# A cross network's last layer: residual rows by DMA transposes instead of TensorE transposes, natural row order, and a new order of the last groups

## The chip, the cores and the metric

One core of a Trainium2 chip runs the kernel. The metric is the device time in microseconds of one execution of the whole program. The kernel was already tuned: TensorE is busy for 99% of the span before the change.

## The reference, cut to what matters

```python
B, F, D, L = 16384, 26, 16, 6          # Din = 416
def reference(x0, ws, bs):             # x0 (16384, 416), ws (6, 416, 416), bs (6, 416), all bf16
    x = x0
    for l in range(6):
        proj = jnp.einsum('bd,de->be', x, ws[l]) + bs[l]
        x = x0 * proj + x
    return x
```

Each layer is a 416x416 matrix product, a multiply by the first input and an addition of the previous x (here called the residual).

## The kernel before

The 16384 rows are eight groups of 2048. A group is held transposed: features on the partitions (three tiles of 128 features, `t` = 0, 1, 2, and a tail of 32), rows in the free dimension (four chunks of 512, `j`). The 48 pairs of group and layer are interleaved, so that one pair's TensorE work hides another's eviction. Groups 0 to 6 finish transposed, are turned by DMA transposes and stored.

The last pair, group 7 layer 5, has nothing behind it to hide its end. It is computed "row-major": the data is the stationary operand, the weights stream, and the result has rows on the partitions, ready to store. It goes in four row blocks `kk` of four 128-row pieces `j`. A block is 4 tail matmuls, 4 bias matmuls and 12 main matmuls into four PSUM banks, an eviction on ScalarE, a multiply and an addition on VectorE. The addition needs the residual in row-major form too, and the kernel before makes it with TensorE transposes:

```python
def turn_main(kp, bks, ts):            # 24 transposes of 128x128 for each pair of row blocks, kp = 0, 1
    for j in range(NJ):
        for h2 in range(2):
            for t in ts:
                o = h2 * CH + t * P
                add("pe", ... h.transpose(psum_t(bks[j])[:, o:o + P], xcol(t, j, kk), ident[:, :]) ...)
def rows_out(kp, bks):                 # copies out of PSUM: j == 0 (and j == 2 of kp 1) on ScalarE, others on VectorE
    ...
def nat_mul(kk, j, b):
    ... ScalarE: on[:, j, kk, :] = PSUM bank b
    ... VectorE: on *= x0 rows          # the last piece: one VectorE operation out of PSUM
def nat_add(kk, j):
    ... VectorE: on += x5n[:, j, kk, :]  # the residual rows
# [... cut ...]
turn_main(0, bka, (0, 1)); turn_tails(0, bka)
nat_rows(0, bkb, True)                  # tail and bias matmuls of block 0
for j in range(NJ): nat_full(0, j, bkb[j], False, (0, 1))
turn_main(0, bka, (2,)); rows_out(0, bka)
layer_full(0, bkb, (2,))                # the rest of block 0, with its multiplies and additions
turn_main(1, bka, (0, 1, 2)); turn_tails(1, bka); rows_out(1, bka)
nat_rows(1, bkb, True); layer_full(1, bkb); nat_store(0, 2, 0, NJ)
# [... blocks 2 and 3 alike, with bka and bkb ...]
```

`add` appends to an engine's queue and derives semaphore waits from what an operation reads and writes. Each queue is filled in the order of the `add` calls. Here `bka` and `bkb` are the two halves of the eight PSUM banks. By those waits a write into a bank starts only when the reader of its old contents is done. (PSUM is the memory that TensorE's results go to; the banks are its eight parts.)

Of the kernel before, what the change touches and what calls it, by code (L numbers as in the profile page):

```python
# [3 lines left out]
P = 128  # L4
# [194 lines left out]
def bass_standalone__cross_network_dcn__recsys_kernel(  # L199
# [18 lines left out]
             (0, 4), (1, 3), (2, 2), (3, 1), (0, 5), (1, 4), (2, 3), (3, 2), (4, 0), (1, 5),  # L218
             (2, 4), (3, 3), (4, 1), (5, 0)]
    order += [(NG - 1 - g, L - 1 - l) for g, l in reversed(order)]  # L220
    order[-6:] = [(5, 5), (7, 3), (6, 4), (7, 4), (6, 5), (7, 5)]
    assert len(set(order)) == NG * L
    cuts = [1, 2, 3, 4, 4, 4, 4, 4, 4, 4, 4, 4, 3, 2]
    batches = []
# [94 lines left out]
    def quad(g, l, j):  # L319
        q = (j + turn_of(g, l)) % NJ  # L320
        return q, slice(q * T32, (q + 1) * T32)
# [194 lines left out]
    def perm(ap, j):  # L516
        return ap[j * CH:(j + 1) * CH, :].rearrange("(p k) f -> p k f", k=KK)
# [28 lines left out]
    def psum_t(b):  # L546
        return psum[:, b * CH:(b + 1) * CH].bitcast(BF16)
# [75 lines left out]
    def load_last():  # L623

        for j in range(NJ):
            add("sp", lambda h, j=j: h.dma_start(x0n7[:, j, :, :], perm(rows7, j)),
                writes=(x0_all(sn) + x03_toks(sn) if j == 0 else []) + [("n7", j)], lane="n7", batch=0)
        for j in range(NJ):
            add("sp", lambda h, j=j: h.dma_start(brow[j * T32:j * T32 + 1, :], bs[L - 1:L, :]),
                writes=[("brow", j)] + (["brow"] if j == 0 else []), lane="brow", batch=0)  # L630

    def output(g):

        s, s3 = xset[(g, L)], xtail[(g, L)]
        def turn(t):
            add("sp", lambda h: h.dma_start_transpose(
                ost[:, :, t * P:(t + 1) * P], xs[s][:, t * GC:(t + 1) * GC]),
                reads=[("x", s, t, j) for j in range(NJ)], writes=[("ost", t)], lane="ot", batch=g)

        turn(0)  # L640
        add("sp", lambda h: h.dma_start_transpose(ot3[:, :, :], x3s[s3][:, :]),
            reads=[("x3", s3)], writes=["ot3"], lane="ot3", batch=g)
        add("pool", lambda h: h.tensor_copy(  # L643
            ost[:, :, NT * P:D].rearrange("p (j k) f -> p j k f", j=NJ),
            ot3[:, :, :].rearrange("p k (j f) -> p j k f", j=NJ)),
            reads=["ot3"], writes=[("ost", NT)])
        turn(1)
        turn(2)
        rows = out[g * GC:(g + 1) * GC, :]
        o = ost[:, :, :].rearrange("p (j k) f -> p j k f", j=NJ)  # L650
        parts = [("(j k p) f -> p j k f", 0, NJ)]
        if g == 0:
            parts = [("(j p k) f -> p j k f", 0, NJ)]
        for pat, j0, j1 in parts:
            add("sp", lambda h, pat=pat, j0=j0, j1=j1: h.dma_start(
                rows[j0 * CH:j1 * CH, :].rearrange(pat, j=j1 - j0, k=KK), o[:, j0:j1, :, :]),
                reads=[("ost", t) for t in range(NT + 1)],
                writes=[("out", g, j0)], lane="out", batch=g)
        free_x.append(s)
        free_3.append(s3)  # L660

    items = []
    where = {(b[min(1, len(b) - 1)], 0): b for b in batches[:-1]}
    where[((LAST - 1, L - 1), 0)] = batches[-1]
    del where[((0, 0), 0)]
    where[((0, 1), 0)] = where.pop(((1, 0), 0))
    tiles = [((1, 0), 0), ((1, 0), 1), ((0, 1), 0), ((0, 1), 1), ((0, 1), 2), ((1, 0), 2)]
# [1 line left out]
    for jb, i in tiles:  # L669
        items.append(("tile", jb, i))  # L670
        if (jb, i) in where:
            items.append(("tails", where[(jb, i)]))

    late = items.index(("tile", (LAST, L - 2), NT - 1))
    items.append(items.pop(late))


    single = 0
# [29 lines left out]
    def finish_tile(g, l, n=1):  # L708
        tiles_done[(g, l)] = tiles_done.get((g, l), 0) + n
        if tiles_done[(g, l)] == NT:  # L710
            done_with(g, l)
# [18 lines left out]
    for n, it in enumerate(items):  # L730
        if it[0] == "tails":
            tails(it[1])
            continue
        _, (g, l), i = it
        if (g, l) not in started:
            start_job(g, l)
        if mode[n] in ("FR", "F1"):
            banks = job_banks()
            full(g, l, i, banks, True, False)
            rows32(g, l, i, banks, False, mode[n] == "F1")  # L740
            evacuate(g, l, i, banks, list(range(NJ)), 2)
        else:
            banks = job_banks()
            rows32(g, l, i, banks, True)
            if n == len(items) - 1:
                full(g, l, i, banks, False, True, lambda j: evacuate(g, l, i, banks, [j], 1))
            else:
                full(g, l, i, banks, False, False)
                evacuate(g, l, i, banks, list(range(NJ)), 2)
        finish_tile(g, l)  # L750


    g, l = LAST, L - 1
# [1 line left out]
    s3, tok3 = x3_src(g, l)  # L755

    def xcol(t, j, kk):
        return src(t, j, j + 1).rearrange("p (m k) -> p m k", k=KK)[:, :, kk]

    def x3col(j, kk):  # L760
        return s3[quad(g, l, j)[1], :].rearrange("p (m k) -> p m k", k=KK)[:, :, kk]

    first_use = {"x5": True, "on": True}

    def turn_main(kp, bks, ts):
        for j in range(NJ):
            for h2 in range(2):
                for t in ts:
                    o = h2 * CH + t * P
                    add("pe", lambda h, j=j, t=t, kk=2 * kp + h2, o=o: h.transpose(  # L770
                        psum_t(bks[j])[:, o:o + P], xcol(t, j, kk), ident[:, :]),
                        reads=[stok(t, j), "ident"], writes=[("ps", bks[j])])

    def turn_tails(kp, bks):
        for h2 in range(2):
            for j in range(NJ):
                r, q = quad(g, l, j)
                o = h2 * CH + NT * P
                add("pe", lambda h, j=j, q=q, r=r, kk=2 * kp + h2, o=o: h.matmul(
                    psum_t(bks[j])[:, o:o + T32], x3col(j, kk), ident[q, q], is_transpose=True,  # L780
                    tile_position=(r * T32, 0)),
                    reads=tok3 + ["ident"], writes=[("ps", bks[j])])

    def rows_out(kp, bks):

        for j in range(NJ):
            extra = x0_all(s5) + x03_toks(s5) if first_use.pop("x5", None) else []
            eng = "act" if j == 0 or (kp and j == 2) else "dve"
            dst = x5n[:, j, 2 * kp:2 * kp + 2, :]
            sp_ = psum_t(bks[j]).rearrange("p (a f) -> p a f", a=2)[:, :, 0:D]  # L790
            if eng == "act":
                add("act", lambda h, dst=dst, sp_=sp_: h.activation(dst, sp_, ACT_F.Copy),
                    reads=[("ps", bks[j])], writes=extra + [("x5n", j, kp)])
            else:
                add("dve", lambda h, dst=dst, sp_=sp_: h.tensor_copy(dst, sp_),
                    reads=[("ps", bks[j])], writes=extra + [("x5n", j, kp)])

    def nat_full(kk, j, b, first, ts=range(NT)):
        for t in ts:
# [33 lines left out]
    def nat_add(kk, j):  # L833
        o, x5v = on[:, j, kk, :], x5n[:, j, kk, :]
        add("dve", lambda h: h.tensor_tensor(o, o, x5v, ALU.add),  # L835
            reads=[("on", j, kk), ("x5n", j, kk // 2)], writes=[("on", j, kk)])

    stores = [0]

    def nat_store(k0, k1, j0, j1, eng="sp"):  # L840
        dst = out[LAST * GC:B, :].rearrange("(j p k) f -> p j k f", j=NJ, k=KK)[:, j0:j1, k0:k1, :]
        add(eng, lambda h: h.dma_start(dst, on[:, j0:j1, k0:k1, :]),
            reads=[("on", j, kk) for j in range(j0, j1) for kk in range(k0, k1)],
            writes=[("out7", k0, j0)], lane=f"out7_{stores[0]}", batch=0)
        stores[0] += 1

    bka, bkb = take(NJ), take(NJ)
# [2 lines left out]
    def layer_full(kk, bks, ts=range(NT)):  # L850
        for j in range(NJ):
            nat_full(kk, j, bks[j], False, ts)
            nat_mul(kk, j, bks[j])
            if kk < last:
                if j:
                    nat_add(kk, j - 1)
            elif j == 1:
                nat_add(kk, 0)
                nat_add(kk, 1)
                nat_store(kk - 1, kk + 1, 0, 2)  # L860
            elif j == 2:
                nat_add(kk, 2)
                nat_store(kk, kk + 1, 2, 3)
        nat_add(kk, NJ - 1)

    turn_main(0, bka, (0, 1))
    turn_tails(0, bka)
    nat_rows(0, bkb, True)
    for j in range(NJ):
        nat_full(0, j, bkb[j], False, (0, 1))  # L870
    turn_main(0, bka, (2,))
    rows_out(0, bka)
    layer_full(0, bkb, (2,))
    turn_main(1, bka, (0, 1, 2))
    turn_tails(1, bka)
    rows_out(1, bka)
    nat_rows(1, bkb, True)
    layer_full(1, bkb)
    nat_store(0, 2, 0, NJ)
    nat_rows(2, bka, True)  # L880
    layer_full(2, bka)
    nat_store(2, 3, 2, NJ)
    nat_rows(3, bkb, True)
    layer_full(3, bkb)
    nat_store(3, 4, 3, NJ, "act")

    pr.emit()

# [27 lines left out]
```

## Time and profile before

| | before |
|---|---|
| median time | 479.14 us at first (3 runs), 479.61 us beside the changed kernel (6 runs, 478.57 to 480.46) |
| span of the profiled execution | 476.7 us |
| TensorE busy | 470.2 us |

From the profile page of the kernel before: the span, the busy time and share of each engine with its instruction count, and the engines' shares of the chain that ended last.

```profile
span 476.7 us, 8467 instructions
...
PE 470.2 (99%) x3403; PEld 198.7 (42%) x3403; DVE 406.9 (85%) x714; ACT 342.4 (72%) x371; POOL 7.2 (2%) x14
...
PE 92%; SPq 4%; DVE 2%; ACT 1%; DMA 0%; issue 0%
```

TensorE is the limit, and only the end of the program is touched by the change. The next lines are from the timeline of the kernel before. The columns are start (us), duration (us), engine, line, operation, output and input, shapes, and count; a bracket would give the idle time before it and what ended it. Several rows are merged into one where the same operation repeats.

```profile
447.02 0.43 PE L471 MATMUL ps<-x,w 32*32 32x512 bf16 x16
...
461.02 0.74 DVE L408 TENSOR_TENSOR x<-tw,x 128x512 bf16<-128x512 bf16 x2
...
462.49 1.52 PEld L770 LDWEIGHTS ps<-ident,x 128*128 128x128 bf16 x24
...
464.65 2.30 PE L800 MATMUL ps<-wm,x 128*128 128x416 bf16 x12
...
473.48 0.58 DVE L825 TENSOR_TENSOR x<-ps,x 128x416 bf16<-128x416 f32 x1
474.09 0.38 DVE L835 TENSOR_TENSOR x<-x,x 128x416 bf16<-128x416 bf16 x1
474.50 0.37 ACTq L842 DMA_DIRECT2D out_dram<-x  x1
```

The first line is the last group of tail tiles. The second is the last chunk of layer 4 leaving VectorE: it ends at 461.76. Only then can the last transposes run. TensorE works through 24 transposes from 462.5 on (the line shown is their weight loads, PEld) and through block 1's 12 main matmuls in 2.30 us. The last multiply of VectorE starts at 473.48, the last addition ends at 474.47, the last store is issued at 474.50, and the span ends at 476.7.

From the windows view of the kernel before: a stretch, its length, busy time and number of operations of each engine, then the granted TensorE clock (1.00 is full speed), the DMA engines' busy share as this view gives it (it can exceed 1) and the rate in GB/s.

```profile
core 0: us, PE busy (x) PEld busy (x) DVE busy (x) ACT busy (x) POOL busy (x), PEclk, DMA share, GB/s
...
462.12:464.35 2.23, 2.23 (x41) 1.89 (x42) 2.23 (x8) 1.81 (x5) 0.00 (x0) 1.00 0.78 162
464.35:467.07 2.72, 2.72 (x24) 1.42 (x20) 2.70 (x9) 2.70 (x6) 0.00 (x0) 1.00 0.72 243
...
469.78:472.50 2.72, 2.60 (x20) 1.28 (x12) 2.47 (x10) 2.00 (x4) 0.00 (x0) 1.00 1.06 372
```

TensorE and VectorE are both full in the first two stretches and at least 90% busy in the third.

### The profile page before, as it was taken

What the parts mean: (1) busy time and instruction counts of PE and PEld (TensorE: products, weight loads), DVE (VectorE), ACT (ScalarE), POOL (GpSimd) and SP (SyncE); (2) the same over time, 40 slices, a digit from 0 to 9 for tenths busy, and PEclk for the clock granted to TensorE, in tenths of its full rate; (3) what the DMA queues carried; (4) which work ended last, traced back from release to release, by engine and by line L of the source; (5) the groups of instructions that cost most, each with busy time, mean ns of one, the idle gap of its engine ahead of it and who ended that gap; (6) DMA issues with size and microseconds to landing.
All of it is one profiled execution on the core that took longest, in us unless ns stands there. A gap on an engine that the chain in (4) does not pass through costs nothing.

```text
span 476.7 us, 8467 instructions
## 1 busy us (share of the span) xinstructions
PE 470.2 (99%) x3403; PEld 198.7 (42%) x3403; DVE 406.9 (85%) x714; ACT 342.4 (72%) x371; POOL 7.2 (2%) x14
## 2 busy tenths in 40 slices
PE   8999999999999999999999999999999999999996
PEld 6344444444444444444444444434444444444353
DVE  2888888888888888898888879888888888888897
ACT  4677777777777777777777777777777777777775
POOL 0000000000000000000000000000000000000000
PEclk9999999999999999999999999999999999999999
DMA  8886920720102477379219932970000138026388
GB/s 232 179 176 144 195 66 1 157 65 1 34 1 46 76 212 156 75 168 242 57 35 211 207 80 40 189 236 0 2 15 21 26 64 231 0 45 159 108 145 286
DMA packets 131851, 52.27 MB, mean 110 GB/s; under 512 B 108122, under 2 KB 130404, under 8 KB 131812
## 3 DMA queue, kind: packets, MB, share of 16 engines
q1 hardware_dynamic: 131064, 51.20, 46.8%
q8 instruction: 26, 0.43, 0.4%
q10 hardware_dynamic: 748, 0.54, 0.3%
q14 instruction: 13, 0.11, 0.1%
HBM read 5.97 MB, written 13.63 MB: 41 GB/s over the span
## 4 chain that ended last, share of the span: by engine, by line
PE 92%; SPq 4%; DVE 2%; ACT 1%; DMA 0%; issue 0%
PE ps L456 75%; PE ps L477 7%; PE ps L497 7%; SPq L292 2%; PE ps L800 1%; PE ps L471 1%; DVE x L408 1%; DVE tw L403 1%; SPq L297 1%; PE ps L488 1%; SPq L285 0%; SPq L521 0%; ACT tw L394 0%; PE ps L770 0%; DMA x<-ost 0%; SPq L304 0%
## 5 line engine op out<-in xcount | busy, mean ns | idle before, releaser
L394 ACT ACTIVATE tw<-ps,bias 128x1024 bf16<-128x1024 f32 (+1 forms) x295 | 299.8, 1071 | 120.0 <-PE ps L477 75.9
L456 PE MATMUL ps<-x,wm 128*128 128x512 bf16 x1692 | 379.4, 379 | 0.0
L456 PEld LDWEIGHTS ps<-x,wm 128*128 128x128 bf16 x1692 | 159.0, 98 | 213.2 <-issue 28.3
L403 DVE TENSOR_TENSOR tw<-tw,x 128x1024 bf16<-128x1024 bf16 (+1 forms) x285 | 192.7, 685 | 53.9 <-ACT tw L394 53.6
L408 DVE TENSOR_TENSOR x<-tw,x 128x1024 bf16<-128x1024 bf16 (+1 forms) x285 | 182.5, 681 | 0.0
L477 PE MATMUL ps<-x,w 32*128 32x512 bf16 x512 | 39.2, 379 | 0.2 <-DMA x<-ost 0.2
L497 PE MATMUL ps<-x,wm 128*32 128x512 bf16 x564 | 33.0, 380 | 0.0
L434 ACT ACTIVATE ts<-ps,bias 128x512 bf16<-128x512 f32 x47 | 28.8, 701 | 0.0
L438 DVE TENSOR_TENSOR x<-ts,x 128x512 bf16<-128x512 bf16 x47 | 18.6, 417 | 3.0 <-DMA x<-x 3.0
L497 PEld LDWEIGHTS ps<-x,wm 128*32 128x32 bf16 x564 | 13.8, 96 | 17.6 <-issue 5.3
L477 PEld LDWEIGHTS ps<-x,w 32*128 32x128 bf16 x512 | 7.8, 92 | 27.9 <-issue 27.1
L436 DVE TENSOR_TENSOR ts<-ts,x 128x512 bf16<-128x512 bf16 x47 | 18.6, 418 | 0.0
L643 POOL COPY ost<-ot 128x512 bf16<-128x512 bf16 x7 | 6.3, 900 | 449.9 <-DMA ot<-x 449.9
L800 PE MATMUL ps<-wm,x 128*128 128x416 bf16 x48 | 9.4, 341 | 0.0
L568 DVE COPY x<-ps 128x512 bf16<-128x512 bf16 x4 | 1.7, 425 | 8.0 <-PE ps L561 8.0
L828 ACT ACTIVATE x<-ps 128x416 bf16<-128x416 f32 x15 | 7.1, 525 | 1.3 <-PE ps L800 1.1
L565 ACT ACTIVATE x<-ps 128x512 bf16<-128x512 bf16 x8 | 4.3, 594 | 4.8 <-PE ps L561 4.8
L800 PEld LDWEIGHTS ps<-wm,x 128*128 128x128 bf16 x48 | 5.1, 115 | 3.8 <-issue 1.4
L488 PE MATMUL ps<-x,w 32*32 32x512 bf16 x188 | 5.9, 374 | 0.0
L830 DVE TENSOR_TENSOR x<-x,x 128x416 bf16<-128x416 bf16 x15 | 5.4, 368 | 0.3 <-ACT x L828 0.2
L471 PE MATMUL ps<-x,w 32*32 32x512 bf16 x208 | 5.6, 385 | 0.0
L835 DVE TENSOR_TENSOR x<-x,x 128x416 bf16<-128x416 bf16 x16 | 5.6, 369 | 0.1
(35 smaller groups left out, 43.2 us busy)
## 6 DMA issues: line engine op xcount, KB each, us to landing
out_dram<-ost SPq DMA_DIRECT2D x7, 1664.0 KB, 6.8
x<-in_x_dram SPq DMA_DIRECT2D x7, 416.0 KB, 7.1
x<-x SPq DMA_DIRECT2D x24, 96.0 KB, 2.2
wm<-in_ws_dram SPq DMA_DIRECT2D x5, 312.0 KB, 3.4
x<-x SPq DMA_DIRECT2D x22, 64.0 KB, 2.0
x<-ost SPq DMA_DIRECT2D x28, 32.0 KB, 2.3
out_dram<-x SPq DMA_DIRECT2D x1, 832.0 KB, 4.3
x<-x SPq DMA_DIRECT2D x24, 32.0 KB, 1.9
```

What stands on the lines that cost most here:

```text
L394: add("act", lambda h, a=a, w=w, b0=b0: h.activation(tw[r][:, a * CH:(a + w) * CH], psum[:, b0 * CH:(b0 + w) * CH], ACT_F.Identity, bias=b ...
L403: add("dve", lambda h, a=a, e=e: h.tensor_tensor(tw[r][:, a * CH:e * CH], tw[r][:, a * CH:e * CH], x0s[s0][:, i * GC + a * CH:i * GC + e * ...
L408: add("dve", lambda h, a=a, e=e: h.tensor_tensor(xs[so][:, i * GC + a * CH:i * GC + e * CH], tw[r][:, a * CH:e * CH], src(i, a, e), ALU.ad ...
L434: add("act", lambda h: h.activation(ts[r][:, :], bank(b), ACT_F.Identity, bias=bias[:, 3, l:l + 1], scale=1.0), reads=[("ps", b), "bias"], ...
L436: add("dve", lambda h: h.tensor_tensor(ts[r][:, :], ts[r][:, :], x03, ALU.mult), reads=[("ts", r)] + tok0, writes=[("ts", r)], release=True)
L438: add("dve", lambda h: h.tensor_tensor(x3s[so][:, :], ts[r][:, :], res, ALU.add), reads=[("ts", r)] + rtok, writes=[("x3", so), ("x3", so, ...
L456: add("pe", lambda h, t=t, j=j: h.matmul(bank(banks[j]), wm[l][:, t, ecols], src(t, j, j + 1), start=(first and t == 0), stop=(not first a ...
L471: add("pe", lambda h, q=q, j=j, r=r, c=c, o=o: h.matmul(psum[o, banks[j] * CH:(banks[j] + 1) * CH], w3[l][q, i * P + c * T32:i * P + (c + ...
L477: add("pe", lambda h, q=q, j=j, r=r: h.matmul(bank(banks[j]), w3[l][q, ecols], src[q, :], start=first, stop=not first, tile_position=(r * ...
L488: add("pe", lambda h, l=l, b=b, s3=s3, ri=ri, qi=qi, ro=ro, qo=qo: h.matmul(psum[qo, b * CH:(b + 1) * CH], w3[l][qi, NT * P:D], s3[qi, :], ...
L497: add("pe", lambda h, t=t, j=j, src=src, l=l, b=b, ro=ro, qo=qo: h.matmul(psum[qo, b * CH:(b + 1) * CH], wm[l][:, t, NT * P:D], src(t, j, ...
L800: add("pe", lambda h, t=t: h.matmul(bank(b, n=D), xcol(t, j, kk), wm[l][:, t, :], start=(first and t == 0), stop=(not first and t == NT - 1)),
```

## The change

Its intent is to take 48 of the 64 transposes off TensorE, and with them most copies out of PSUM. DMA transposes bring residual tiles 0 and 1 and the tail; only tile 2, which is ready last, stays on TensorE. DMA transposes deliver natural row order, so the last layer's rows are no longer interleaved by four. The order of the last groups goes back to the general rule, which finishes group 6 earlier, so that its own DMA transposes leave the sync queue before those of the residual (called turns below), while its store waits until after them.

```diff
-    order[-6:] = [(5, 5), (7, 3), (6, 4), (7, 4), (6, 5), (7, 5)]
...
+    def rest_tail():                      # called from output(6), between its turns
+        add("sp", lambda h: h.dma_start_transpose(ot5, x3s[s3][:, :]), ...)
+        # two GpSimd copies ot5 -> x5n[..., NT * P:D]; the first also claims the buffer
+    def rest_turn(t):                     # after tiles 0 and 1 of group 7, layer 4
+        add("sp", lambda h: h.dma_start_transpose(
+            x5f[:, :, t * P:(t + 1) * P], xs[s][:, t * GC:(t + 1) * GC]),
+            reads=[("x", s, t, j) for j in range(NJ)] + [("x5n", 0, NT)], ...)
...
+        if (g, l) == (LAST, L - 2) and i < NT - 1:
+            rest_turn(i)
+            if i:
+                store(LAST - 1)           # group 6's store, now behind the turns
...
     def xcol(t, j, kk):
-        return src(t, j, j + 1).rearrange("p (m k) -> p m k", k=KK)[:, :, kk]
+        return src(t, j, j + 1)[:, kk * P:(kk + 1) * P]
...
-    turn_main(0, bka, (0, 1))
-    turn_tails(0, bka)
-    nat_rows(0, bkb, True)
+    nat_rows(0, bka, True)
     for j in range(NJ):
-        nat_full(0, j, bkb[j], False, (0, 1))
-    turn_main(0, bka, (2,))
-    rows_out(0, bka)
-    layer_full(0, bkb, (2,))
-    turn_main(1, bka, (0, 1, 2))
-    turn_tails(1, bka)
-    rows_out(1, bka)
+        nat_full(0, j, bka[j], False, (0, 1))
+    for j in range(NJ):
+        turn_last(j, bkb[j // 2])         # tile 2: four transposes, two pieces to a bank
+        nat_full(0, j, bka[j], False, (2,))
+        nat_mul(0, j, bka[j])
+        if j % 2:
+            last_out(j - 1, bkb[j // 2])  # PSUM copies: j = 0, 1 on ScalarE, 2, 3 on VectorE
+            last_out(j, bkb[j // 2])
     nat_rows(1, bkb, True)
     layer_full(1, bkb)                    # now also carries block 0's additions, block 2 block 1's and its own
-    nat_store(0, 2, 0, NJ)                # two row blocks together, 1664 bytes a row
+    nat_store(0, 0, NJ)                   # one row block, 832 bytes a row
```

More of the change, by code (lines that the diff above doesn't have):

```diff
@@ L625, in load_last @@
         for j in range(NJ):
-            add("sp", lambda h, j=j: h.dma_start(x0n7[:, j, :, :], perm(rows7, j)),
+            add("sp", lambda h, j=j: h.dma_start(
+                x0n7[:, j, :, :], rows7[j * CH:(j + 1) * CH, :].rearrange("(k p) f -> p k f", k=KK)),
                 writes=(x0_all(sn) + x03_toks(sn) if j == 0 else []) + [("n7", j)], lane="n7", batch=0)
@@ L646, in output, with store @@
             reads=["ot3"], writes=[("ost", NT)])
+        if g == LAST - 1:
+            rest_tail()
         turn(1)
         turn(2)
+        if g < LAST - 1:
+            store(g)
+        free_x.append(s)
+        free_3.append(s3)
+    def store(g):
         rows = out[g * GC:(g + 1) * GC, :]
@@ L658, in output @@
                 writes=[("out", g, j0)], lane="out", batch=g)
-        free_x.append(s)
-        free_3.append(s3)
+    x5f = x0s[s5][:, 0:XW + CH].rearrange("p (a f) -> p a f", f=D)
+    def rest_tail():
+        s3 = xtail[(LAST, L - 1)]
+        hold = free_x.pop()
+        ot5 = xs[hold][:, 0:CH].rearrange("p (k f) -> p k f", k=KK)
+        held = ("x", hold, 0, 0)
+        add("sp", lambda h: h.dma_start_transpose(ot5, x3s[s3][:, :]),
+            reads=[("x3", s3)], writes=[held], lane="ot5", batch=0)
+        n = turn_of(LAST, L - 1)
+        staged = ot5.rearrange("p k (q f) -> p q k f", q=NJ)
+        for j0, j1 in ((0, NJ - n), (NJ - n, NJ)):
+            if j0 < j1:
+                q0 = (j0 + n) % NJ
+                add("pool", lambda h, j0=j0, j1=j1, q0=q0: h.tensor_copy(
+                    x5n[:, j0:j1, :, NT * P:D], staged[:, q0:q0 + j1 - j0, :, :]),
+                    reads=[held], writes=[("x5n", j, NT) for j in range(j0, j1)] +
+                    (x0_all(s5) + x03_toks(s5) if j0 == 0 else []))
+    def rest_turn(t):
+        s = xset[(LAST, L - 1)]
+        add("sp", lambda h: h.dma_start_transpose(
+            x5f[:, :, t * P:(t + 1) * P], xs[s][:, t * GC:(t + 1) * GC]),
+            reads=[("x", s, t, j) for j in range(NJ)] + [("x5n", 0, NT)],
+            writes=[("x5n", j, t) for j in range(NJ)], lane=f"x5_{t}", batch=0)
     items = []
     where = {(b[min(1, len(b) - 1)], 0): b for b in batches[:-1]}
-    where[((LAST - 1, L - 1), 0)] = batches[-1]
+    where[((LAST - 1, L - 1), 1)] = batches[-1]
     del where[((0, 0), 0)]
@@ L672, in bass_standalone__cross_network_dcn__recsys_kernel @@
             items.append(("tails", where[(jb, i)]))
-    late = items.index(("tile", (LAST, L - 2), NT - 1))
-    items.append(items.pop(late))
     single = 0
@@ L757, in xcol @@
     def xcol(t, j, kk):
-        return src(t, j, j + 1).rearrange("p (m k) -> p m k", k=KK)[:, :, kk]
+        return src(t, j, j + 1)[:, kk * P:(kk + 1) * P]
     def x3col(j, kk):
-        return s3[quad(g, l, j)[1], :].rearrange("p (m k) -> p m k", k=KK)[:, :, kk]
-    first_use = {"x5": True, "on": True}
-    def turn_main(kp, bks, ts):
-        for j in range(NJ):
-            for h2 in range(2):
-                for t in ts:
-                    o = h2 * CH + t * P
-                    add("pe", lambda h, j=j, t=t, kk=2 * kp + h2, o=o: h.transpose(
-                        psum_t(bks[j])[:, o:o + P], xcol(t, j, kk), ident[:, :]),
-                        reads=[stok(t, j), "ident"], writes=[("ps", bks[j])])
@@ L774, in turn_tails @@
-    def turn_tails(kp, bks):
-        for h2 in range(2):
-            for j in range(NJ):
-                r, q = quad(g, l, j)
-                o = h2 * CH + NT * P
-                add("pe", lambda h, j=j, q=q, r=r, kk=2 * kp + h2, o=o: h.matmul(
-                    psum_t(bks[j])[:, o:o + T32], x3col(j, kk), ident[q, q], is_transpose=True,
-                    tile_position=(r * T32, 0)),
-                    reads=tok3 + ["ident"], writes=[("ps", bks[j])])
-    def rows_out(kp, bks):
-        for j in range(NJ):
-            extra = x0_all(s5) + x03_toks(s5) if first_use.pop("x5", None) else []
-            eng = "act" if j == 0 or (kp and j == 2) else "dve"
-            dst = x5n[:, j, 2 * kp:2 * kp + 2, :]
-            sp_ = psum_t(bks[j]).rearrange("p (a f) -> p a f", a=2)[:, :, 0:D]
-            if eng == "act":
-                add("act", lambda h, dst=dst, sp_=sp_: h.activation(dst, sp_, ACT_F.Copy),
-                    reads=[("ps", bks[j])], writes=extra + [("x5n", j, kp)])
-            else:
-                add("dve", lambda h, dst=dst, sp_=sp_: h.tensor_copy(dst, sp_),
-                    reads=[("ps", bks[j])], writes=extra + [("x5n", j, kp)])
+        return s3[quad(g, l, j)[1], kk * P:(kk + 1) * P]
@@ new lines, in bass_standalone__cross_network_dcn__recsys_kernel, with turn_last, last_out @@
+    first_use = {"on": True}
+    def turn_last(j, b):
+        t, o = NT - 1, (j % 2) * CH
+        for kk in range(KK):
+            add("pe", lambda h, kk=kk: h.transpose(
+                psum_t(b)[:, o + kk * P:o + (kk + 1) * P], xcol(t, j, kk), ident[:, :]),
+                reads=[stok(t, j), "ident"], writes=[("ps", b)])
+    def last_out(j, b):
+        dst = x5n[:, j, :, (NT - 1) * P:NT * P]
+        sp_ = psum_t(b)[:, (j % 2) * CH:(j % 2 + 1) * CH].rearrange("p (k f) -> p k f", k=KK)
+        kw = dict(reads=[("ps", b), ("x5n", 0, NT)], writes=[("x5n", j, NT - 1)])
+        if j < 2:
+            add("act", lambda h: h.activation(dst, sp_, ACT_F.Copy), **kw)
+        else:
+            add("dve", lambda h: h.tensor_copy(dst, sp_), **kw)
@@ L835, in nat_add, with nat_store @@
         add("dve", lambda h: h.tensor_tensor(o, o, x5v, ALU.add),
-            reads=[("on", j, kk), ("x5n", j, kk // 2)], writes=[("on", j, kk)])
+            reads=[("on", j, kk)] + [("x5n", j, t) for t in range(NT + 1)], writes=[("on", j, kk)])
     stores = [0]
-    def nat_store(k0, k1, j0, j1, eng="sp"):
-        dst = out[LAST * GC:B, :].rearrange("(j p k) f -> p j k f", j=NJ, k=KK)[:, j0:j1, k0:k1, :]
-        add(eng, lambda h: h.dma_start(dst, on[:, j0:j1, k0:k1, :]),
-            reads=[("on", j, kk) for j in range(j0, j1) for kk in range(k0, k1)],
-            writes=[("out7", k0, j0)], lane=f"out7_{stores[0]}", batch=0)
+    def nat_store(kk, j0, j1, eng="sp"):
+        dst = out[LAST * GC:B, :].rearrange("(j k p) f -> p j k f", j=NJ, k=KK)[:, j0:j1, kk, :]
+        add(eng, lambda h: h.dma_start(dst, on[:, j0:j1, kk, :]),
+            reads=[("on", j, kk) for j in range(j0, j1)],
+            writes=[("out7", kk, j0)], lane=f"out7_{stores[0]}", batch=0)
         stores[0] += 1
@@ L854, in layer_full @@
             if kk < last:
-                if j:
+                nat_add(kk - 1, j)
+                if kk == 2 and j:
                     nat_add(kk, j - 1)
@@ L859, in layer_full @@
                 nat_add(kk, 1)
-                nat_store(kk - 1, kk + 1, 0, 2)
+                nat_store(kk, 0, 2)
             elif j == 2:
                 nat_add(kk, 2)
-                nat_store(kk, kk + 1, 2, 3)
-        nat_add(kk, NJ - 1)
-    turn_main(0, bka, (0, 1))
-    turn_tails(0, bka)
-    nat_rows(0, bkb, True)
-    for j in range(NJ):
-        nat_full(0, j, bkb[j], False, (0, 1))
-    turn_main(0, bka, (2,))
-    rows_out(0, bka)
-    layer_full(0, bkb, (2,))
-    turn_main(1, bka, (0, 1, 2))
-    turn_tails(1, bka)
-    rows_out(1, bka)
+                nat_store(kk, 2, 3)
+        if kk > 1:
+            nat_add(kk, NJ - 1)
+    nat_rows(0, bka, True)
+    for j in range(NJ):
+        nat_full(0, j, bka[j], False, (0, 1))
[6 more added lines that the diff above has]
+            last_out(j, bkb[j // 2])
     nat_rows(1, bkb, True)
     layer_full(1, bkb)
-    nat_store(0, 2, 0, NJ)
+    nat_store(0, 0, NJ)
     nat_rows(2, bka, True)
     layer_full(2, bka)
-    nat_store(2, 3, 2, NJ)
+    nat_store(1, 0, NJ)
+    nat_store(2, 0, NJ)
     nat_rows(3, bkb, True)
     layer_full(3, bkb)
-    nat_store(3, 4, 3, NJ, "act")
+    nat_store(3, 3, NJ, "act")
     pr.emit()
```

## The prediction

> **What bounds the kernel now.** TensorE: busy 470.2 of 476.7 us (page, busy times), and the chain of waits is PE for 92%. The change touches the last 30 us. The timeline and the chain show there:
>
> - The last tile of group 7, layer 4 leaves VectorE in four chunks, landing at 460.1, 460.8, 461.4 and 461.8 us. From 454.3 to 461.4 the chain is VectorE.
> - TensorE then runs without a gap from 462.1 to 472.4: 0.70 us for the rest of row block 0, 1.5 us for the other half of the transposes, then three blocks of 2.7 us (12 matmuls 2.24, tail and bias rows 0.48).
> - VectorE is full over the same stretch (about 0.285 us per 128x416 operation). Its last multiply starts at 473.5, 1.1 us after TensorE ended; last add 474.1 to 474.5; last store issues at 474.5 and ends the span at 476.7.
>
> **Removed.** 32 main transposes (0.056 us each in a row: 1.8 us) and 16 tail ones (0.35 us); eight 128x832 copies out of PSUM: five on VectorE (2.6 us), three on ScalarE (2.5 us).
>
> **Added.** Three DMA transposes on the sync queue (about 2.2, 2.2 and 1.2 us of queue), two small GpSimd copies, four 128x512 copies (0.55 us on ScalarE, 0.43 on VectorE, as this shape takes at the start). Last stores use 832-byte rows instead of 1664.
>
> **What is critical.** If only TensorE counted, row block 1 would start at about 462.3 instead of 464.35: 2 us gained. I expect none of it. Block 1 reuses the two PSUM banks that hold the last transposes. Its first row matmul waits for two ScalarE copies, its second for the VectorE copies, which stand behind the fourth multiply of block 0, which waits for ScalarE's sixth operation. Adding durations: ScalarE finishes at about 463.6, VectorE multiplies and copies until 464.7, so block 1 starts then and TensorE ends at about 472.6, 0.2 us later than before. The additions of block 0 moved too: block 2 now carries 12 VectorE operations (3.4 us) against 2.7 us of TensorE, so the last addition moves from 474.5 to about 475.0.
>
> Then the DMAs. The turns queue behind two other turns: the second should issue at about 461.5 and land at about 466, when the first addition needs it (466.5). Stores of blocks 1 and 2 (832 KB) now issue at about 472, where DMA already moved 340 to 370 GB/s (windows): 0.4 us more before the last store lands, an estimate. The two extra GpSimd copies fall near 457. The Trainium skill ("SBUF — State Buffer", section "SBUF: two separate sides") says that a GpSimd operation and a VectorE operation with two SBUF inputs block each other; the trace agrees: two additions took 1.70 us beside the GpSimd copy of 457.3, 1.29 elsewhere. Estimate 0.3 us.
>
> **Sum.** About +0.5 (compute), +0.3 (port), +0.4 (stores): 480.3 us, range 477.6 to 482.4. Faster by over 2%: 1%; within 2%: 98%; slower: 1%.
>
> **What would show it.** TensorE waiting 2 us or more at the second row matmul of block 1, released by the VectorE copy; VectorE idle before its fourth multiply of block 0; last multiply starting over 2 us after TensorE's end; store of group 6 issued after 463. Wrong if that wait is under 1 us: then 477.5 or less.
>
> **What would make it wrong.** Copies finishing sooner; turns landing after 468; the new order opening gaps before 455.

## The result, and the profile after

The changed kernel took 482.24 us (median of 6 runs, 481.27 to 483.70) against 479.61 us before (6 runs). The ratio is 1.0057, with a 95% interval of 1.0037 to 1.0077: about 2.7 us slower.

The same parts of the profile page, changed kernel:

```profile
span 480.5 us, 8377 instructions
...
PE 470.2 (98%) x3355; PEld 195.7 (41%) x3355; DVE 405.3 (84%) x711; ACT 341.4 (71%) x370; POOL 8.7 (2%) x16
...
PE 91%; SPq 4%; DVE 3%; ACT 1%; DMA 0%; issue 0%
```

TensorE has 48 matmuls fewer and the same busy time. That is the first hint that something ran slower. The timeline of the changed kernel at the end:

```profile
447.53 0.43 PE L470 MATMUL ps<-x,w 32*32 32x512 bf16 x16
...
461.86 0.75 DVE L407 TENSOR_TENSOR x<-tw,x 128x512 bf16<-128x512 bf16 x2
...
463.81 0.34 PE L829 MATMUL ps<-w,x 32*128 32x416 bf16 x1 [0.52 <-ACT x L812]
464.20 0.79 DVE L848 TENSOR_TENSOR x<-x,x 128x416 bf16<-128x416 bf16 x2 [1.01 <-ACT x L846]
464.90 0.75 DVE L814 COPY x<-ps 128x512 bf16<-128x512 bf16 x2
...
465.71 0.53 PE L829 MATMUL ps<-w,x 32*128 32x416 bf16 x3 [1.55 <-DVE x L814]
...
466.52 3.50 PE L818 MATMUL ps<-wm,x 128*128 128x416 bf16 x12
...
477.59 0.38 DVE L853 TENSOR_TENSOR x<-x,x 128x416 bf16<-128x416 bf16 x1
478.00 0.37 ACTq L860 DMA_DIRECT2D out_dram<-x  x1
```

The last chunk of layer 4 ends at 462.61. TensorE finishes its transposes and block 0 at 463.3, waits 0.52 us for the ScalarE copies, runs one row matmul, then waits 1.55 us for the VectorE copies (bracket of the line at 465.71). VectorE in turn stood idle for 1.01 us behind its multiplies (464.20), because they waited for ScalarE. Then block 1's 12 main matmuls take 3.50 us, where the same 12 took 2.30 before. The windows view of the changed kernel for these three stretches, and below them two half-microsecond stretches:

```profile
463.30:465.71 2.41, 0.35 (x2) 0.10 (x3) 1.42 (x4) 1.28 (x3) 0.00 (x0) 0.98 1.27 95
465.71:466.58 0.87, 0.87 (x8) 0.19 (x9) 0.00 (x0) 0.00 (x0) 0.00 (x0) 0.50 1.28 286
466.58:470.02 3.44, 3.44 (x17) 1.48 (x20) 1.32 (x4) 1.52 (x3) 0.00 (x0) 0.64 1.14 326
...
465.30:465.80 0.50, 0.09 (x4) 0.10 (x7) 0.35 (x2) 0.00 (x0) 0.00 (x0) 0.82 0.74 165
...
468.80:469.30 0.50, 0.50 (x3) 0.25 (x2) 0.19 (x1) 0.49 (x1) 0.00 (x0) 0.77 1.04 351
```

Over the 2.41 us between the end of block 0 and 465.71 TensorE was busy for 0.35 us. After it the granted clock is 0.50, and it stays there until about 469, when it returns to 1.00. (The clock changes within the two short stretches; from their means of 0.82 and 0.77 the changes are estimated at about 465.6 and 469.0.) The profiles of e3 and e7, which keep these waits, show the same: waits of 0.52 and 1.55 us, then a clock of 0.50, and 3.89 and 3.95 us for block 1's 12 main matmuls.

The sync queue of the changed kernel, and VectorE's first multiply of block 1 with the first residual addition behind it:

```profile
455.86 4.99 SPq L636 DMA_TRANSPOSE ost<-x  x2
460.96 5.53 SPq L690 DMA_TRANSPOSE x<-x  x2
466.54 0.59 SPq L663 DMA_DIRECT2D out_dram<-ost  x1
```

```profile
468.32 0.38 DVE L848 TENSOR_TENSOR x<-x,x 128x416 bf16<-128x416 bf16 x1 [2.67 <-ACT x L846]
468.62 0.37 DVE L853 TENSOR_TENSOR x<-x,x 128x416 bf16<-128x416 bf16 x1
```

The view of the turns' source line gives the time from issue to landing:

```profile
DMA to landing us min/median/max: 5.5/5.6/5.7
```

The second residual turn was issued at 462.9 and so landed at about 468.5, and group 6's store was issued at 466.54. The first addition, which needs that turn, starts at 468.62. TensorE's late block 1 and the late turn meet at the same moment. A single profile can't tell which of the two holds the end; the experiments can.

Profiles differ at the start. The first twelve tail matmuls of 32 columns began at 18.6 us in the profile before, at 18.7 in the one after, and at 21.2 to 22.3 in four of the experiments (e4, e6, e8, e10), although none of the edits touches an instruction ahead of them; in the others at 18.5 to 20.1. In the late ones TensorE waited for one of the first loads (0.80 us in e4, 0.87 in e6, 1.87 in e8, 2.15 in e10; the profile before shows no such wait), and in e8 and e10 the granted clock then was 0.50 for about 3.4 us. Why the loads came later is open. At the mark the profiles differ by up to 3.5 us (447.02 to 450.51), as much as the effect. So I compare the end from the time mark (start of the last tail tiles) on. All columns are differences of times in the timeline, one profiled execution per kernel, us after the mark (the span is given to 0.1 us, so the last two columns are good to about that):

| kernel | last chunk ready | TensorE ends | last addition ends | span ends | last addition to span end |
|---|---|---|---|---|---|
| before | 14.74 | 25.36 | 27.45 | 29.68 | 2.23 |
| after | 15.08 | 27.85 | 30.44 | 32.97 | 2.53 |
| e1 warm | 15.08 | 26.28 | 28.91 | 31.73 | 2.82 |
| e2 copies first | 15.08 | 24.54 | 28.91 | 31.72 | 2.81 |
| e3 turns early | 15.07 | 27.91 | 30.50 | 32.98 | 2.48 |
| e4 both | 15.06 | 24.53 | 27.50 | 30.13 | 2.63 |
| e5 order only | 14.68 | 25.62 | 27.71 | 29.98 | 2.27 |
| e6 natural rows only | 14.74 | 25.22 | 27.31 | 29.78 | 2.47 |
| e7 GpSimd copies held | 14.67 | 27.55 | 30.14 | 32.62 | 2.48 |
| e8 combined | 14.74 | 24.53 | 27.13 | 29.66 | 2.53 |
| e9 free banks first | 14.75 | 24.03 | 26.76 | 29.23 | 2.47 |
| e10 stores split | 14.75 | 24.03 | 26.81 | 29.29 | 2.48 |

The loss from the mark on is 32.97 - 29.68 = 3.29 us.

### The profile page after: what moved, and what is told of

The parts are those of the page before. It is cut to its first block, busy times and chain, and to the rows that moved or that the text cites. A ratio compares the mean times of both kernels' runs of the same rounds, so it can differ in the third digit from the quotient of the medians.

```text
span 480.5 us, 8377 instructions
## 1 busy us (share of the span) xinstructions
PE 470.2 (98%) x3355; PEld 195.7 (41%) x3355; DVE 405.3 (84%) x711; ACT 341.4 (71%) x370; POOL 8.7 (2%) x16
## 4 chain that ended last, share of the span: by engine, by line
PE 91%; SPq 4%; DVE 3%; ACT 1%; DMA 0%; issue 0%
PE ps L455 74%; PE ps L476 7%; PE ps L496 7%; SPq L291 2%; PE ps L470 1%; PE ps L818 1%; DVE x L407 1%; DVE x L853 1%; DVE tw L402 1%; SPq L296 1%; PE ps L487 1%; DVE x L848 1%; SPq L520 0%; SPq L284 0%; ACT tw L393 0%; ACT x L846 0%
## 5 line engine op out<-in xcount | busy, mean ns | idle before, releaser
L437 DVE TENSOR_TENSOR x<-ts,x 128x512 bf16<-128x512 bf16 x47 | 18.7, 419 | 3.7 <-DMA x<-x 3.6
L435 DVE TENSOR_TENSOR ts<-ts,x 128x512 bf16<-128x512 bf16 x47 | 18.6, 419 | 0.0
L818 PE MATMUL ps<-wm,x 128*128 128x416 bf16 x48 | 11.2, 372 | 0.1
```

Source lines behind the costliest of these rows:

```text
L435: add("dve", lambda h: h.tensor_tensor(ts[r][:, :], ts[r][:, :], x03, ALU.mult), reads=[("ts", r)] + tok0, writes=[("ts", r)], release=True)
L437: add("dve", lambda h: h.tensor_tensor(x3s[so][:, :], ts[r][:, :], res, ALU.add), reads=[("ts", r)] + rtok, writes=[("x3", so), ("x3", so, ...
L818: add("pe", lambda h, t=t: h.matmul(bank(b, n=D), xcol(t, j, kk), wm[l][:, t, :], start=(first and t == 0), stop=(not first and t == NT - 1)),
```

## The experiments

Theory A: the wait for the two PSUM banks, with the slow clock that follows it, is the whole loss. Theory B: behind it stands a second wall, the landing of the second residual turn, so that removing either alone gains little. Rivals: late turns alone; DMA traffic slowing the matmuls; the new order; the short store rows. All ten results were correct. Each experiment has 5 or 6 runs, the kernel before 11 in the same rounds.

| kernel | median, us | before, same rounds | ratio (95% interval) |
|---|---|---|---|
| e1 warm | 481.22 | 478.79 | 1.0053 (1.0026 to 1.0080) |
| e2 copies first | 481.74 | 478.79 | 1.0061 (1.0038 to 1.0084) |
| e3 turns early | 482.36 | 478.79 | 1.0068 (1.0043 to 1.0093) |
| e4 both | 480.27 | 478.79 | 1.0023 (0.9997 to 1.0048) |
| e5 order only | 479.06 | 479.04 | 1.0001 (0.9989 to 1.0013) |
| e6 natural rows only | 479.51 | 479.04 | 1.0018 (1.0001 to 1.0036) |
| e7 GpSimd copies held | 481.48 | 479.04 | 1.0050 (1.0037 to 1.0063) |
| e8 combined | 479.74 | 479.04 | 1.0019 (1.0006 to 1.0032) |
| e9 free banks first | 479.35 | 479.13 | 0.9997 (0.9975 to 1.0020) |
| e10 stores split | 478.61 | 479.13 | 0.9992 (0.9968 to 1.0016) |

The times alone do not separate e1, e2 and e3 from the changed kernel (ratio 1.0057, interval 1.0037 to 1.0077, in other rounds). Only e4 of the four lies lower, and even its interval overlaps. So what is said below of one or two microseconds rests on one profile of each kernel, read from the mark.

### e1: dummy matmuls in the wait

```diff
+    for _ in range(12):
+        add("pe", lambda h: h.matmul(bank(bkb[2], n=D), ident[:, :], wm[l][:, 0, :], start=True, stop=True),
+            reads=["ident", ("wm", l)], writes=[("ps", bkb[2])])
     nat_rows(1, bkb, True)
```

> The changed kernel plus 12 dummy 128x416 matmuls (0.187 us each, about 2.24 us) into a free PSUM bank while TensorE would wait for the PSUM copies. Result stays correct. Theory A (the idle time of about 2.2 us on TensorE lowers the granted clock, and that is why block 1 took 3.44 us instead of 2.24): the wait for the VectorE copy is filled, block 1's 12 matmuls take 2.2 to 2.4 us again and the granted clock reads 1.00 there; the span shortens by up to 1.2 us, less if the additions then wait for the residual turns, which land at about 468.5. Rival (the matmuls are slow because the DMA transposes run beside them): block 1 still takes about 3.4 us and the time is unchanged.

The windows view from the end of TensorE's wait on, TensorE's dummies (the line numbers are this kernel's) and block 1 in the timeline, and VectorE's first and last addition:

```profile
465.65:468.40 2.75, 2.75 (x23) 1.28 (x27) 0.64 (x2) 1.53 (x3) 0.00 (x0) 1.00 1.17 283
```

```profile
463.07 2.27 PE L897 MATMUL ps<-wm,ident 128*128 128x416 bf16 x12
...
466.11 2.28 PE L818 MATMUL ps<-wm,x 128*128 128x416 bf16 x12
```

```profile
468.13 0.38 DVE L853 TENSOR_TENSOR x<-x,x 128x416 bf16<-128x416 bf16 x1 [0.36 <-DMA x<-x]
...
476.01 0.37 DVE L853 TENSOR_TENSOR x<-x,x 128x416 bf16<-128x416 bf16 x1
```

With work in the gap the clock stays at 1.00 and block 1 takes 2.28 us, although the DMA engines were as busy as in the changed kernel (share 1.17). So DMA traffic does not slow the matmuls, and idle time lowered the clock: that is shown. TensorE's end moves from 27.85 to 26.28 after the mark, 1.57 us. These are 1.2 us in the 12 matmuls and 0.4 us in the row and bias matmuls ahead of them (0.87 us in the changed kernel, 0.46 here). The last addition moves by nearly the same, 1.53 us. But the first addition, at 468.13, now waited 0.36 us for the DMA: the second wall is close. The end of the span gains only 1.24 us, because the stretch from the last addition to it is 2.82 us here and 2.53 in the changed kernel, with the same stores.

### e2, e3, e4: the copies, the turns, and both

```diff
 # e2: the PSUM copies ahead of block 0's evictions and multiplies
         nat_full(0, j, bka[j], False, (2,))
-        nat_mul(0, j, bka[j])
         if j % 2:
             last_out(j - 1, bkb[j // 2])
             last_out(j, bkb[j // 2])
+    for j in range(NJ):
+        nat_mul(0, j, bka[j])
 # e3: in output(), group 6 alone: its second turn ahead of the two tail turns
         turn(0)
+        if g == LAST - 1:
+            turn(1)
```

e4 has both edits.

> The changed kernel with the four PSUM copies of the last transposes placed ahead of block 0's evictions and multiplies on ScalarE and VectorE. Theory A (the wait for these copies, plus the slow clock after it, is all the loss): TensorE waits under 1 us instead of 2.1, block 1 runs at full clock, TensorE ends about 2.9 us earlier and the whole kernel is about 2.9 us faster than the changed one, near 479.3. Theory B (behind that wait stands a second one, the landing of the second residual turn at about 468.5): TensorE ends about 2.9 us earlier, but VectorE's first addition still starts at about 468.5 and the kernel gains only about 1 us, near 481.2.

> The changed kernel with the second turn of group 6 issued ahead of the two tail turns, so that both residual turns issue and land 2 to 2.5 us earlier (about 466). Theory A and B alike: no change on its own (within 0.5 us of the changed kernel, 482.2), because the first addition stands behind a multiply that TensorE's late block 1 feeds at 468.3. Rival (late residual turns are the cause of the loss): 2 us faster.

> Both of the former two edits. Theory B: the two walls fall together, the gain is larger than the sum of the single ones: about 3 to 3.5 us faster than the changed kernel, 478.7 to 479.3, about level with the kernel before (479.6). Theory A: same as copies first alone. If neither matters, 482.2.

e2: TensorE's second wait and block 1, then VectorE around the first addition, and its last.

```profile
464.72 0.35 PE L829 MATMUL ps<-w,x 32*128 32x416 bf16 x3 [0.40 <-DVE x L814]
...
465.18 2.28 PE L818 MATMUL ps<-wm,x 128*128 128x416 bf16 x12
```

```profile
466.47 0.38 DVE L848 TENSOR_TENSOR x<-x,x 128x416 bf16<-128x416 bf16 x1 [0.50 <-ACT x L846]
468.92 0.37 DVE L853 TENSOR_TENSOR x<-x,x 128x416 bf16<-128x416 bf16 x1 [2.08 <-DMA x<-x]
...
476.81 0.38 DVE L853 TENSOR_TENSOR x<-x,x 128x416 bf16<-128x416 bf16 x1
```

TensorE's wait fell from 1.55 to 0.40 us, block 1 runs at full speed, and TensorE ends 3.31 us earlier after the mark (24.54 against 27.85). VectorE gained half of that, 1.53 us. Its first addition waited 2.08 us for the DMA. Theory A expected 2.9 us at the end and falls, in the profile (1.25 us) and in the times (ratio at least 1.0038, where theory A's 479.3 us would be about the time of the kernel before). That the fix gains about 1 us, as theory B has it, only the profile shows; the median of 481.74 us and the ratio of 1.0061 do not. The end of the kernel could not be told from TensorE's end.

e3: the two residual turns on the sync queue, and the multiply and the first addition on VectorE.

```profile
457.64 4.75 SPq L693 DMA_TRANSPOSE x<-x  x2
```

```profile
467.59 0.38 DVE L851 TENSOR_TENSOR x<-x,x 128x416 bf16<-128x416 bf16 x1 [2.35 <-ACT x L849]
467.88 0.37 DVE L856 TENSOR_TENSOR x<-x,x 128x416 bf16<-128x416 bf16 x1
```

From the mark the turns were issued 2.9 us earlier than in the changed kernel (457.64 - 447.12 = 10.52 against 460.96 - 447.53 = 13.43), but the addition still stands directly behind a multiply that block 1 feeds late. The end did not move (32.98 after the mark, 32.97 in the changed kernel). Late turns alone are not the cause either. (The edit also brings group 6's store forward, from 19.0 to 15.3 us after the mark; that did not move the end.)

e4: VectorE's first addition and its last.

```profile
468.61 0.38 DVE L856 TENSOR_TENSOR x<-x,x 128x416 bf16<-128x416 bf16 x1 [0.68 <-DMA x<-x]
...
476.49 0.38 DVE L856 TENSOR_TENSOR x<-x,x 128x416 bf16<-128x416 bf16 x1
```

This profile started late (its mark is at 449.37, against 447.53 in the changed kernel). From the mark, the last addition ends at 27.50, 2.94 us before the changed kernel and level with the kernel before (27.45). Single gains after the mark, in span end: e2 1.25 us, e3 none, both 2.84 us. The two walls stood one behind the other, as theory B has it. A 0.68 us wait for the DMA remains. e4's median agrees in direction but not in full: 480.27 us is above the 478.7 to 479.3 that I expected. Part of that is the late start, which the profile shows (2.35 us against the kernel before); how the unprofiled runs divide is open.

### e5, e6: one part of the change alone

```diff
 # e5, on the kernel before
-    order[-6:] = [(5, 5), (7, 3), (6, 4), (7, 4), (6, 5), (7, 5)]
-    where[((LAST - 1, L - 1), 0)] = batches[-1]
+    where[((LAST - 1, L - 1), 1)] = batches[-1]
-    late = items.index(("tile", (LAST, L - 2), NT - 1))
-    items.append(items.pop(late))
 # e6, on the kernel before: rows of a block in natural order, one store per row block
-        return src(t, j, j + 1).rearrange("p (m k) -> p m k", k=KK)[:, :, kk]
+        return src(t, j, j + 1)[:, kk * P:(kk + 1) * P]
-        dst = out[LAST * GC:B, :].rearrange("(j p k) f -> p j k f", j=NJ, k=KK)[:, j0:j1, k0:k1, :]
+        dst = out[LAST * GC:B, :].rearrange("(j k p) f -> p j k f", j=NJ, k=KK)[:, j0:j1, kk, :]
```

> The kernel before with the new order of the last groups alone (residual rows still turned on TensorE, rows still interleaved by four). Theory B: the order costs nothing, because the number of matmuls and the structure of the last tiles are the same: within 0.5 us of the kernel before, granted clock 1.00. Rival (the interleaved order opens gaps): 1 us slower or more.

> The kernel before with the natural row order alone: each partition stores one row of 832 bytes at a time instead of 1664 where two row blocks go together. Theory B: the time from the last addition to the end of the span grows by at most 0.5 us from 2.2, the rest is unchanged: 0 to 0.5 us slower. Rival (short store rows are most of the loss): 2 us slower.

The new order costs nothing that the times resolve (ratio 1.0001, interval 0.9989 to 1.0013); from the mark it is 0.3 us. The natural rows leave the last addition where it was (27.31 against 27.45) and lengthen the time from there to the end of the span from 2.23 to 2.47 us, 0.24 us. The changed kernel shows 2.53. By the times the natural rows alone are 0.2% slower (1.0018, interval 1.0001 to 1.0036), but two of the six runs lie at 481.4 us and the others at 478.8 to 479.7, and the profiled run, one of those two, started late; so that figure need not be the row order's cost.

### e7: the GpSimd copies held

```diff
-                    reads=[held], writes=[("x5n", j, NT) ...] + (claim of the buffer)
+                    reads=[held, ("x5n", 0, "claim"), ("x", s, NT - 1, NJ - 1)], writes=[("x5n", j, NT) ...]
+        # a one-column memset on GpSimd claims the buffer; the copies are added after the last tile
```

> The changed kernel with the two GpSimd copies of the residual tail held until the last chunk of layer 4 has left VectorE. Theory (they share a port with VectorE): the VectorE operations around 457 to 460, 1.40 us a pair in the changed kernel, go back to about 1.2 to 1.3 us, so the last chunk is ready about 0.3 us earlier relative to the last tail tiles; the end gains no more than that, near 0.3 us, which the times will hardly resolve. Rival (no shared port): pairs stay at 1.40 us.

The GpSimd copies in the changed kernel, VectorE beside them there, and the same two VectorE groups in e7:

```profile
457.11 1.66 POOL L683 COPY x<-x 128x256 bf16<-128x256 bf16 x2 [0.54 <-DMA x<-x]
```

```profile
457.04 1.48 DVE L402 TENSOR_TENSOR tw<-tw,x 128x1024 bf16<-128x1024 bf16 x2
458.44 1.48 DVE L407 TENSOR_TENSOR x<-tw,x 128x1024 bf16<-128x1024 bf16 x2
```

```profile
456.78 1.28 DVE L402 TENSOR_TENSOR tw<-tw,x 128x1024 bf16<-128x1024 bf16 x2
457.99 1.28 DVE L407 TENSOR_TENSOR x<-tw,x 128x1024 bf16<-128x1024 bf16 x2
```

Two groups go from 1.48 to 1.28 us each (from start to start 1.40 and 1.21, the figure that the expectation uses). The last chunk is ready 0.41 us earlier after the mark (14.67 against 15.08) and the span ends 0.35 us earlier. The Trainium skill, "SBUF — State Buffer", section "SBUF: two separate sides", says that a GpSimd operation and a VectorE operation with two SBUF inputs hold a shared port pair against each other for the whole instruction; these numbers agree that the two collide, and don't test whether the hold is exclusive.

### e8, e9, e10: towards a version that beats both

```diff
 # e8 = e2 and e7, and: all turns of group 6 ahead of the tail turns, all four PSUM copies on ScalarE,
-        if kk == KK - 1 and j == NJ - 1:             # nat_mul: straight out of PSUM
+        if kk == 0 or (kk == KK - 1 and j == NJ - 1):
 # and block 0's additions one piece later
 # e9 = e8, and block 1 begins with the two banks that the transposes never used
-    nat_rows(1, bkb, True)
-    layer_full(1, bkb)
+    for js in ((2, 3), (0, 1)):
+        nat_rows(1, bkb, True, js)
+        for j in js: nat_full(1, j, bkb[j], False); nat_mul(1, j, bkb[j]); ...
 # e10 = e9, and the stores of blocks 1 and 2 in halves
```

> Copies first and turns early together with more: group 6's turns all ahead of the tail turns, the four PSUM copies on ScalarE, block 0 multiplied straight out of PSUM on VectorE, the first additions one step later, the GpSimd tail copies held. Theory B: VectorE has fewer gaps after the last chunk, the last addition ends about 1 us earlier than in the kernel before, relative to the last tail tiles; stores take 0.4 us of it back. 0.5 to 1 us faster than before (ratio 0.998 to 0.999). If the residual turns still land late, about level with before.

> The combined kernel, and block 1 takes its row groups in the order 2, 3, 0, 1, so that its first matmuls go into the two PSUM banks that the last transposes never used. Theory B: TensorE's remaining wait of about 1 us before block 1 falls to 0.3 us or less; the last addition ends 26.1 to 26.6 us after the last tail tiles (27.1 in the combined kernel, 27.45 before), if the residual turns land in time; 0.5 to 1 us faster than before in that stretch, ratio near 0.998. If the turns' landing is the next wall, VectorE waits there and the end stays near 27.1.

> The same, and the stores of blocks 1 and 2 go out by halves, each as soon as its additions are done. Expected: the time from the last addition to the end of the span falls from 2.5 us back to about 2.2 us, the rest as in the former run. Rival (the last store's landing does not depend on the stores queued ahead of it): stays at 2.5 us.

e8 missed: the last addition ends 0.32 us before that of the kernel before, not 1 us, and the store takes it back (29.66 against 29.68). The ratio is 1.0019. e9 took away TensorE's wait before block 1 (TensorE ends at 24.03 instead of 24.53), and VectorE's line shows what then came first, beside its last addition:

```profile
467.06 0.38 DVE L869 TENSOR_TENSOR x<-x,x 128x416 bf16<-128x416 bf16 x1 [0.77 <-DMA x<-x]
...
474.66 0.37 DVE L869 TENSOR_TENSOR x<-x,x 128x416 bf16<-128x416 bf16 x1
```

The first addition waits 0.77 us for the turn again. From the mark, e9 ends 0.45 us before the kernel before (29.23 against 29.68). The time does not resolve that: ratio 0.9997, interval 0.9975 to 1.0020. e10 is alike (0.9992), and its split stores did not shorten the last stretch (2.48 us): the expectation of 2.2 us failed. That does not clear the stores queued ahead: e1 and e2 have the changed kernel's rows and stores, and their last stretch is 2.8 us. The last store of 104 KB took 1.7 us to land in the kernel before, 1.9 in e6, 2.0 in the changed kernel and 2.3 in e1 and e2; in the 3 us before its issue the DMA engines moved 274 GB/s in the changed kernel and 326 in e1. So other traffic may well be part of it, beside the row order; neither is shown to be the cause. No version is shown to be faster than the kernel before.

## Why the prediction was right or wrong

The measured 482.24 us lies inside the range (477.6 to 482.4), at its edge. It was slower, by under 2%, as forecast. The central 480.3 us was 1.9 us too low: the prediction had a loss of 1.2 us (480.3 against 479.14), and the pair of medians shows 2.6. That the measured time still lies inside is partly luck: the range happened to be wide enough for a term that the prediction did not have, the slow clock.

- **"Block 1 reuses the two PSUM banks that hold the last transposes"**: right. TensorE waits 0.52 and 1.55 us there, released by the ScalarE and the VectorE copies, and VectorE stands idle for 1.01 us before its third multiply of block 0 (I had said the fourth). The wait for the second row matmul alone was 1.55 us by the timeline, below the 2 us that I named; both waits together are 2.07.
- **"TensorE ends at about 472.6, 0.2 us later than before"**: wrong, and the largest error. It ended 2.49 us later after the mark (27.85 against 25.36). I costed block 1 with the durations of a full clock and left out what an idle TensorE does to its clock. e1 measures that term: 1.57 us. The rest is the later last chunk, 0.34 us, and a wait somewhat longer than my sum (about 0.6 us for the remainder, not taken apart).
- **"The second should issue at about 461.5 and land at about 466"**: mis-sized. It was issued at 462.9 and landed at about 468.5. I had added up issue times of turns in a less crowded queue: the two of group 6 took 4.99 us of queue, the two new ones 5.53. In the changed kernel the late and slow block 1 hid this. e2 uncovers it: a wait of 2.08 us.
- **"The last addition moves from 474.5 to about 475.0"** (and 0.3 for the port): measured 2.99 us later after the mark (30.44 against 27.45). This follows from the two terms above; e4 removes both and brings it to 27.50.
- **Port, 0.3 us**: right; the last chunk came 0.34 us later, and e7 gave 0.41 back.
- **Stores, 0.4 us**: about the right size, 0.3 us; the reason is open. I blamed stores that queue ahead of the last one. Splitting them changed nothing, and the natural row order alone lengthened the last stretch by 0.24 us; but in e1 and e2 the stretch is 0.3 us longer again with the same rows and stores.
- **"Last multiply starting over 2 us after TensorE's end"**: it was 1.6 us (476.97 against 475.38), because TensorE ended later than I thought. **"Store of group 6 issued after 463"**: right, 466.54.
- **The new order opening gaps**: it did not (e5).

So the change took about 1.8 us of transposes and 0.35 us of tail transposes (the prediction's count) off TensorE and lost more than that in this order: a wait for PSUM banks and a slow clock after it. Behind both stood a DMA, for which VectorE waits as soon as TensorE is faster.

## What to carry to other kernels

When work leaves the bottleneck engine, check what its removal leaves in its place: here the removed transposes had stood where ScalarE and VectorE were emptying PSUM banks, and without them the engine waited and then ran at half clock. Cost a wait on TensorE with the clock after it, not only with its own length. When a fix gains less than the engine it frees, look for the next wait in the trace before judging it: here one fix gained 1.25 us, the other none, and the two together 2.84 us.

## What the Trainium skill lacked or had wrong

- "TensorE: Matmul & The Clock Gate", the table of "Why this matters for your kernels", advises no idle gaps above about 3 us between matmul bursts. In the changed kernel two waits of 0.52 and 1.55 us, with 0.35 us of work in 2.41 us, were followed by a granted clock of 0.50 for about 3.4 us (465.6 to 469.0 us); e3 and e7 show it again. The half-speed clock and its length agree with the page's window of about 3.4 us; the safe gap that this row names was too long here. (The page's "A second HAM failure mode: psum-queue depth-cycling" does report frequent short idles that throttle the clock, but gives no length.) In e2, with one wait of 0.40 us in that place, the clock stayed at 1.00. At the start of the program, waits of 1.87 and 2.15 us (e8, e10) were followed by a clock of 0.50 for about 3.4 us too, one of 1.31 us (e9) was not.
- "DMA: Bandwidth & Descriptors" gives a bandwidth for DMA transposes (261 GB/s for a non-contiguous form, in its "Latency and other measured facts") but no time to landing for one that stands in a queue of several. The runs show a median of 4.5 us from issue to landing for the 21 turns of the outputs before the change and 5.6 us for the two residual turns behind two others.
- "DMA: Bandwidth & Descriptors", section "Specifications", names 512 bytes as the least piece for line rate. Here, with both sizes above that, stores of 832-byte rows where there had been 1664, one row block to a store, came with 0.24 us more from the last addition to the end of the span (e6, one profile). That run changes the length of the rows, their order in memory and the number of stores together, and the very last store had 832-byte rows before too, so it does not show that the page's figure is wrong.
